# Attention, SoLU mixture and top-1 experts on one core: gate-and-scale factors made with the weight scales, gathers moved behind the second product, two weight buffers kept free

## The chip, the cores and the metric

One core of one Trainium2 chip runs the whole program. The metric is the time of one execution in device microseconds. Three timed runs of the kernel before are at hand, and one profiled execution.

## What is computed

Three layers follow each other. The change touches the third alone.

```python
# 1: attention within chunks of 64 positions, 4 x 8 heads, 576 positions, head size 64
attn = exp(scores - max) / sum;  out = attn @ v
# 2: h = x @ w_in; solu = h * softmax(h); layer norm over 1024 columns, times g_ln; @ w_out
# 3: top-1 mixture of 8 experts over 2304 tokens of 512 columns
logits = x @ w_gate;  expert = argmax(logits);  gate = softmax(logits)[expert]
h = maximum(x_e @ w1[e], 0)        # up to 576 tokens of expert e, 512 -> 1024
y = h @ w2[e]                      # 1024 -> 512
out[token] = gate[token] * y       # tokens over the capacity of 576 stay zero
```

## The kernel before

**Layers 1 and 2** go over 18 tiles of 128 tokens. A planner (class `Plan`) writes out their order from costs and due times. The change leaves this part alone; in the profiled execution it ends at about 376 us. It has put the tokens, already normalized, in a table `xrows` in device memory, and the list of each expert's tokens with their gate values in `idx_sb` (its float view is `gm`).

**Layer 3** goes over 16 weight matrices in the order of `mats`: w1 of experts 0 and 1, w2 of experts 0 and 1, and then w1 and w2 of each expert from 2 to 7. The loop at L1515 takes them one after the other; a turn with w1 is called the *first product* of its expert, and one with w2 its *second product*. The order within a turn is the order in which the code is written, on each engine for itself. An engine goes through its own list in order, and waits on semaphores for the others.

A matrix of 2 MB is handled in four quarters of 512 KB, in buffers that are handed round in a list `free`:

- `load_q` (L1272) takes a free buffer and loads a quarter into it, on SP's queue.
- `norm_q` (L1281) squares and sums a quarter, the even ones on ACT (L1046), the odd ones on DVE (L1044).
- `fin_q` (L1284) adds the four sums up with a small matmul, reduces the result on DVE (`nst`, L136) and makes the scale from it on POOL (`nsb` and `sw`, L141 and L142).
- `split_q` (L1289) splits a quarter into two f16 parts: ACT writes the high part (L1292) into a free buffer, and DVE then writes the low part beside it (L1293), reading the raw quarter and the high part. The raw buffer goes back to `free` after this.

`job` (L1302) says how far ahead each step may run, and that a load is made only where the list holds at least two buffers, so that one is left for the splits. Within a turn, `work(p)` (L1506) asks for the splits of the matrix two turns later, its scale, and the sums of the one three turns later.

**A first product** (L1531 to L1536) runs `emit_span` over the expert's first 256 tokens, in four groups of 24 matmuls with 256 columns (L1398). ACT takes each group's result (`hA`, L1404) and DVE makes its low part (L1405). The second group doesn't start before both have read the first. Further tiles of 128 tokens follow in `emit_b`, under tests of the expert's count of tokens.

**A second product** (L1518 to L1530) has these pieces, in this order:

1. `fetch_all(e + 2)` for experts 2 to 5: for each tile of 128 tokens of the expert after the next a gather on POOL (L1371) from `xrows` into one of four buffers `xga` and `xgb`, and a transposing DMA on SP (L1376) from there. The tiles from the third on stand under tests of the count.
2. `ffac(e)` (L1472), on POOL: gate value times the two matrices' scales for each token of the expert, in `ff`.
3. `emit_d(e, 0)`: 24 matmuls for the first 128 tokens (L324); ACT scales the result by `ff` into `y` (L1460), and POOL scatters its rows to the output (L1461).
4. `work(p)`.
5. `emit_d` for the further tiles, under tests; a last tile of at most 64 rows is scaled on DVE (L1456, L1457).

Then the turn's four weight buffers are released, and up to eight quarters are loaded (L1537, L1538).

Of the kernel before, what the change touches and what calls it, by code (L numbers as in the profile page):

```python
# [23 lines left out]
def attn_solu_top1_moe(  # L24
# [19 lines left out]
    E = w_gate.shape[1]  # L44
# [27 lines left out]
    def small(name, w=1, dtype=F32, bufs=None):  # L72
        return sm.tile([128, w], dtype, tag=name, name=name, **({"bufs": bufs} if bufs else {}))
# [42 lines left out]
    def bank_tile(slot, name):  # L116
        return psp.tile([128, 512], F32, tag=slot, name=name)
# [16 lines left out]
    def tot_reduce(ar):  # L134
        t = small("nst", bufs=8)
        DVE.tensor_reduce(t, ar, AX.X, ALU.add)  # L136
        return t

    def pow_scale(ss, cst, so):
        b = small("nsb", bufs=8)  # L140
        POOL.tensor_scalar(b, ss, 1.0 / cst ** 2, 1e-36, ALU.mult, ALU.add)  # L141
        POOL.tensor_tensor(so, b.to_broadcast([128, 2]), pexp[:, 0:2], ALU.pow)  # L142
# [67 lines left out]
    NORMS = 7  # L210
# [264 lines left out]
    mats = [(0, 0), (0, 1), (1, 0), (1, 1)]  # L475
# [771 lines left out]
    with tc.manual_schedule():  # L1247
# [20 lines left out]
        free = [spare]  # L1268
        raw_q = {(p, qi): raw_m[p][:, qi * WQ:(qi + 1) * WQ] for p in range(3, 7) for qi in range(NQ)}
# [14 lines left out]
        def fin_q(p, qi):  # L1284
            ar = bank_tile("o", "tot")[:, 0:NQ]
            PE.matmul(ar, ones_f, am[:, p, :], start=True, stop=True)
            pow_scale(tot_reduce(ar), CW, sw[:, p, :])

        def split_q(p, qi):  # L1289
            r, s = raw_q.pop((p, qi)), sw[:, p, 0:1]  # L1290
            w = wm_q[p, qi] = free.pop(0).bitcast(F16).rearrange("p (a f) -> p a f", a=2)
            ACT.activation(w[:, 0], r, AF.Copy, scale=s)  # L1292
            DVE.scalar_tensor_tensor(w[:, 1], r, s, w[:, 0], ALU.mult, ALU.subtract)  # L1293
            free.append(r)
# [7 lines left out]
        def job(kind, p, n=1):  # L1302
            for _ in range(n):
                if not todo[kind]:
                    return
                at = todo[kind][0]
                before = todo.get(needs[kind])
                if at[0] >= p + ahead[kind] or (before and before[0][0] <= at[0] and kind != "N"):
                    return
                if kind == "N" and at not in raw_q or kind == "L" and len(free) < 2:  # L1310
                    return
                steps[kind](*todo[kind].pop(0))

        def need(p):
            for kind in "NFS":
                while todo[kind] and todo[kind][0][0] <= p:
                    steps[kind](*todo[kind].pop(0))
# [4 lines left out]
        def release(p):  # L1322
            if p < 3:
                t = wm[p].rearrange("p a f -> p (a f)").bitcast(F32)
                free.extend(t[:, qi * WQ:(qi + 1) * WQ] for qi in range(NQ))
            else:
                free.extend(wm_q.pop((p, qi)).rearrange("p a f -> p (a f)").bitcast(F32) for qi in range(NQ))
# [5 lines left out]
        def fetch_from(e, j, end=NTJ):  # L1333
            if j < end:
                with tc.If(units(e, 2 * j)):
                    fetch(e, j)
                    fetch_from(e, j + 1, end)

        def emit_from(step, e, j, p, end=NTJ):
            if j < end:  # L1340
                with tc.If(units(e, 2 * j)):
                    hT = hT_of(e, j, step)
                    if step is emit_b and e < 2:
                        fetch(e, j)
                    if rows(j) <= 64:
                        step(e, j, p, hT, True)
                    else:
                        with tc.If(units(e, 2 * j + 1)) as full:
                            step(e, j, p, hT, False)
                            emit_from(step, e, j + 1, p, end)  # L1350
                        with full.Else():
                            step(e, j, p, hT, True)
# [6 lines left out]
        def fetch(e, j, again=False):  # L1359
            col, r = e * NTJ + j, rows(j)  # L1360
            xg = xg_n()
            if again:
                xT = bp.tile([128, 2, FF], F16, tag="hc", name="gxTr").rearrange("p a f -> p (a f)")
                xT = xT[:, 0:2 * KD * r].rearrange("p (k c) -> p k c", k=2 * KD)
            elif e < 2:
                xT = gx[e][:, j - 2, 0:2 * KD * r].rearrange("p (k c) -> p k c", k=2 * KD)
            elif j < 2:
                xT = gx[e][:, :, 128 * j:128 * j + 128]
            else:
                xT = bp.tile([128, 2 * KD, r], F16, tag=f"gxT{j}", name=f"gxT{j}")  # L1370
            POOL.indirect_dma_start(  # L1371
                out=xg[0:r, :], out_offset=None, in_=xrows[:, :],
                in_offset=bass.IndirectOffsetOnAxis(ap=idx_sb[0:r, col, 0:1], axis=0),
                bounds_check=NT, oob_is_err=False,
            )
            SP.dma_start_transpose(out=xT, in_=xg[0:r].bitcast(F16))  # L1376
            xT_m[e, j] = xT
# [4 lines left out]
        def fetch_all(e):  # L1382
            gx[e] = bp.tile([128, 2 * KD, 256], F16, tag="gxA", name="gxA")
            fetch(e, 0)
            fetch(e, 1)
            fetch_from(e, 2)
# [54 lines left out]
        def emit_d(e, j, p, hT, half):  # L1441
            col, r = e * NTJ + j, 64 if half else rows(j)
            op = bank_tile(f"tr{tr_n()}", "op2")
            y = bp.tile([128, DM], F32, tag="y", name="y")[0:r]
            s = ff[0:r, col:col + 1]
            if half:
                h = KF // 2
                if j < 2:
                    lhs = lambda a, kk: hT[:, a * KF + kk, 0:64]
                else:  # L1450
                    hT = hT.rearrange("p k c -> p (k c)")[:, 0:KF * 128].rearrange("p (k c) -> p k c", k=KF)
                    lhs = lambda a, kk: hT[:, a * h + kk % h, kk // h * 64:kk // h * 64 + 64]
                mm_half([op[0:64], op[64:128]], lhs, h, weights(p), DM, (0, 0), (range(h), range(h, KF)))
                t = bp.tile([128, 2, FF], F16, tag="hc", name="yt").rearrange("p a f -> p (a f)").bitcast(F32)[0:64, 0:DM]
                ACT.copy(t, op[64:128])
                DVE.tensor_scalar(y, op[0:64], s, None, ALU.mult)  # L1456
                DVE.scalar_tensor_tensor(y, t, s, y, ALU.mult, ALU.add)  # L1457
            else:
                mm3([(op[0:r], 0)], hT, KF, weights(p), DM, DM)
                ACT.activation(y, op[0:r], AF.Copy, scale=s)  # L1460
            POOL.indirect_dma_start(  # L1461
                out=out_v[col], out_offset=bass.IndirectOffsetOnAxis(ap=idx_sb[0:r, col, 0:1], axis=0),
                in_=y, in_offset=None, bounds_check=NT - 1, oob_is_err=False,
            )
# [6 lines left out]
        def ffac(e):  # L1471
            POOL.tensor_scalar(ff[:, e * NTJ:(e + 1) * NTJ], gm[:, e * NTJ:(e + 1) * NTJ, 1],  # L1472
                               sw[:, mats.index((0, e)), 1:2], sw[:, mats.index((1, e)), 1:2], ALU.mult, ALU.mult)

        fetch_all(2)
        ffac(0)
        job("S", 2, 4)
        job("L", 2, 1)
        y = bp.tile([128, DM], F32, tag="y", name="ye")
# [26 lines left out]
        def work(p):  # L1506
            job("S", p, NQ)
            job("F", p)
            job("N", p, NQ)
            job("S", p, NQ)  # L1510
# [4 lines left out]
        for p in range(2, NM):  # L1515
            a, e = mats[p]
            need(p)
            if a == 1:  # L1518
                if 1 < e < E - 2:
                    fetch_all(e + 2)  # L1520
                if p > 2:
                    ffac(e)
                if p > 2:
                    emit_d(e, 0, p, hT_m[e, 0], False)
                work(p)
                emit_from(emit_d, e, 1, p)
                if e == 0:
                    spill(1)
                    emit_from(emit_b, 1, 2, 1)
                    release(1)  # L1530
            else:  # L1531
                hA = bp.tile([128, 2 * KF, 256], F16, tag="hA", name="hA", bufs=1)
                hT_m[e, 0], hT_m[e, 1] = hA[:, :, 0:128], hA[:, :, 128:256]
                emit_span(gx[e], 256, p, hA)
                work(p)
                emit_from(emit_b, e, 2, p)  # L1536
            release(p)  # L1537
            job("L", p, 2 * NQ)  # L1538
# [27 lines left out]
```

## Time and profile before

| | us |
|---|---|
| timed runs | 698.91, 695.51, 696.09 |
| median | 696.09 |
| time of the profiled execution | 694.92 |
| its span, from the first to the last instruction | 693.2 |
| TensorE busy | 525.2 (76% of the span) |
| VectorE, ScalarE, GpSimd busy | 381.1, 308.8, 271.9 |
| layer 3, from the first gather to the end | 377 to 693 |

Times within the trace count from the start of the span. Engines are written PE (matmul), DVE, ACT, POOL and SP; SPq and POOLq are the DMA issues of these two. In a row of the timeline stand start, duration, engine, line and operation, the output and its inputs by the program's names, and how many instructions the row takes together; in brackets, how long the engine had been idle before it, and what ended that. Layer 3's turns can be told by their matmuls: L1398 with `gxA` is a first product, L324 with `hA` the start of a second one. The tokens are spread unevenly: expert 2 has one tile of 128 tokens, expert 4 has five tiles.

### The profile page before, as it was taken

Reading aid. Unit: us, or ns where it says so; the run is one execution under the profiler, and the core shown is the slowest. Engines: PE = TensorE matmul, PEld = TensorE weight load, DVE = VectorE, ACT = ScalarE, POOL = GpSimd, SP = SyncE. Lnnn points to the kernel's source line nnn. Section 1 sums busy time; section 2 is a strip of 40 time slices with the busy share of each in tenths; the row PEclk is TensorE's granted clock in tenths of the full one; section 3 lists DMA queues with packets and bytes.
Section 4 is the critical chain, followed back from the end, with each engine's and each line's share of the span. In section 5 each row is a group of like instructions: output and inputs, shape, how many; then the busy total and the mean of one; then the engine's idle time right before and its main releaser. Section 6 shows DMA issues by size and latency. Waiting matters only on the chain. (4 is left out here: it accounts for less than half of the span.)

```text
span 693.2 us, 12254 instructions
## 1 busy us (share of the span) xinstructions
PE 525.2 (76%) x4428; PEld 313.9 (45%) x4428; DVE 381.1 (55%) x654; ACT 308.8 (45%) x510; POOL 271.9 (39%) x429
## 2 busy tenths in 40 slices
PE   6567897979899898998778575615838787578794
PEld 6444443534454454444577334314424336254541
DVE  4887978857477456848775324522634323636210
ACT  1556866536575555447422332432534332625110
POOL 1465657542568555667552211110504111513001
PEclk9657999999999999999979798867969899889998
DMA  8993699999975755443554495383271750602021
GB/s 187 341 222 61 125 226 225 235 246 249 191 143 112 138 107 112 95 100 78 188 146 136 108 352 184 110 167 122 69 252 62 162 136 18 139 9 40 11 61 39
DMA packets 186395, 98.84 MB, mean 143 GB/s; under 512 B 167519, under 2 KB 167519, under 8 KB 185920
## 3 DMA queue, kind: packets, MB, share of 16 engines
q1 hardware_dynamic: 180624, 87.23, 52.5%
q0 software_dynamic: 3824, 10.38, 4.6%
q8 instruction: 51, 0.84, 0.5%
q10 hardware_dynamic: 1856, 0.06, 0.2%
q14 instruction: 40, 0.33, 0.1%
HBM read 61.80 MB, written 9.63 MB: 103 GB/s over the span
## 5 line engine op out<-in xcount | busy, mean ns | idle before, releaser
L324 PE MATMUL op<-w_out,uT 128*128 128x512 f16 x432 | 100.1, 390 | 11.1 <-DMA uT<-uc 8.1
L324 PE MATMUL hp<-w_in,xT 128*128 128x512 f16 x432 | 98.3, 385 | 4.9 <-DVE eh L738 2.6
L1398 PE MATMUL hp<-gxA,rawm 128*128 128x256 f16 x360 | 54.4, 293 | 52.9 <-DVE hA L1405 49.0
L1461 POOL DMA_INDIRECT out_dram<-y,idx_sb x20 | 22.9, 1144 | 131.0 <-ACT y L1460 83.0
L324 PEld LDWEIGHTS <-uT 128*128 128x128 f16 x432 | 42.5, 100 | 63.0 <-DMA uT<-uc 9.1
L324 PEld LDWEIGHTS <-xT 128*128 128x128 f16 x432 | 42.0, 99 | 53.7 <-issue 5.2
L1398 PEld LDWEIGHTS <-rawm 128*128 128x128 f16 x360 | 37.6, 105 | 62.5 <-issue 51.7
L1405 DVE SCALAR_TENSOR_TENSOR hA<-hp,hA 128x512 f16<-128x512 f32 x24 | 16.6, 691 | 62.9 <-ACT hA L1404 62.7
L1404 ACT ACTIVATE hA<-hp 128x512 f16<-128x512 f32 x24 | 14.3, 597 | 70.6 <-PE hp L1398 70.1
L1293 DVE SCALAR_TENSOR_TENSOR rawm<-rawm,sw 128x1024 f16<-128x1024 f32 x21 | 27.0, 1284 | 33.0 <-ACT rawm L1292 33.0
L141 POOL TENSOR_SCALAR nsb<-nst 128x1 f32<-128x1 f32 x19 | 8.3, 436 | 89.9 <-DVE nst L136 86.1
L324 PEld LDWEIGHTS <-hA 128*128 128x128 f16 x240 | 23.7, 102 | 35.6 <-issue 9.0
L1398 PEld LDWEIGHTS <-wm 128*128 128x128 f16 x264 | 26.2, 115 | 22.5 <-issue 16.8
L1398 PE MATMUL hp<-gxA,wm 128*128 128x256 f16 x168 | 27.7, 294 | 10.6 <-DVE hA L1405 10.6
L1292 ACT ACTIVATE rawm<-rawm,sw 128x1024 f16<-128x1024 f32 x21 | 24.0, 1145 | 23.8 <-DVE rawm L1293 12.3
L324 PE MATMUL op<-wm,hA 128*128 128x512 f16 x126 | 30.3, 392 | 5.0 <-issue 3.8
L765 POOL TENSOR_TENSOR uc<-eh,uc 128x1024 f16<-128x1024 f32 x13 | 28.4, 2186 | 12.6 <-ACT uc L760 12.6
L1460 ACT ACTIVATE y<-op,ff 128x512 f32<-128x512 f32 x15 | 10.1, 680 | 48.4 <-POOL ff L1472 24.8
L1044 DVE SCALAR_TENSOR_TENSOR dumpv<-rawm 128x1024 f16<-128x1024 f32 x22 | 28.7, 1303 | 4.0 <-DMA rawm<-in_moe_w_dram 3.7
L760 ACT CAST uc<-eh 128x1024 f16<-128x1024 f32 x18 | 18.8, 1045 | 24.1 <-POOL eh L756 11.4
L324 PE MATMUL op<-rawm,hA 128*128 128x512 f16 x114 | 28.2, 396 | 0.6 <-ACT hA L1404 0.6
L142 POOL TENSOR_TENSOR sx<-nsb,pexp 128x2 f32<-128x2 f32 x36 | 27.3, 759 | 3.0
(270 smaller groups left out, 1175.5 us busy)
## 6 DMA issues: line engine op xcount, KB each, us to landing
rawm<-in_moe_w_dram SPq DMA_DIRECT2D x46, 512.0 KB, 5.3
wm<-in_moe_w_dram SPq DMA_DIRECT2D x17, 512.0 KB, 5.3
vt<-in_v_dram SPq DMA_DIRECT2D x72, 64.0 KB, 2.8
xrows<-xr SPq DMA_DIRECT2D x18, 256.0 KB, 2.8
qt<-in_q_dram SPq DMA_DIRECT2D x16, 256.0 KB, 3.7
kt<-in_k_dram SPq DMA_DIRECT2D x16, 256.0 KB, 4.6
rawd<-in_moe_w_out_dram SPq DMA_DIRECT2D x8, 512.0 KB, 5.2
rawd<-in_moe_w_in_dram SPq DMA_DIRECT2D x3, 1024.0 KB, 7.4
```

What stands on the lines that cost most here:

```text
L142: POOL.tensor_tensor(so, b.to_broadcast([128, 2]), pexp[:, 0:2], ALU.pow)
L324: PE.matmul(pp, xT[:, a * K + kk, :], wslice(w, b_, kk * N + f0, n0), start=(kk == 0 and a == 0 and b_ == 0), stop=(kk == K - 1 and a == 1),)
L760: ACT.copy(uc[:, 0, :], st["eh", t])
L765: eng.tensor_tensor(uc[:, 1, :], st.pop(("eh", t)), uc[:, 0, :], ALU.subtract)
L1044: DVE.scalar_tensor_tensor(dumpv, r, 1.0, r, ALU.mult, ALU.mult, accum_out=acc)
L1292: ACT.activation(w[:, 0], r, AF.Copy, scale=s)
L1293: DVE.scalar_tensor_tensor(w[:, 1], r, s, w[:, 0], ALU.mult, ALU.subtract)
L1398: PE.matmul(hp[:, m, :], wslice(weights(p), b_, kk * FF + (i * g + m) * 128, 128), xT[:, a * KD + kk, :], start=(kk == 0 and b_ == 0 and a ...
L1404: ACT.activation(hi, hp, AF.Relu)
L1405: DVE.scalar_tensor_tensor(h[:, KF + i * g:KF + (i + 1) * g, :], hp, 0.0, hi, ALU.max, ALU.subtract)
L1460: ACT.activation(y, op[0:r], AF.Copy, scale=s)
L1461: POOL.indirect_dma_start(out=out_v[col], out_offset=bass.IndirectOffsetOnAxis(ap=idx_sb[0:r, col, 0:1], axis=0), in_=y, in_offset=None, b ...
```

## The change

Three edits, all in layer 3.

1. The factors are made as soon as the second matrix's scale is there: `fin_q` calls `ffac` behind `pow_scale`. For the matrices whose scales come from the planner's part (experts 0, 1 and 2) the factors are made together at the start. The call of `ffac` in the second product goes.
2. `fetch_all(e + 2)` is called at the end of the second product, behind the last tile, and no more at its start.
3. A load is made only where three buffers are free, so that two are left.

```diff
@@ fin_q
             pow_scale(tot_reduce(ar), CW, sw[:, p, :])
+            if mats[p][0]:
+                ffac(mats[p][1])
@@ job
-                if kind == "N" and at not in raw_q or kind == "L" and len(free) < 2:
+                if kind == "N" and at not in raw_q or kind == "L" and len(free) < 3:
                     return
@@ before the loop
         fetch_all(2)
-        ffac(0)
+        for p in range(2, NORMS):
+            if mats[p][0]:
+                ffac(mats[p][1])
@@ the loop, second product
             if a == 1:
-                if 1 < e < E - 2:
-                    fetch_all(e + 2)
-                if p > 2:
-                    ffac(e)
                 if p > 2:
                     emit_d(e, 0, p, hT_m[e, 0], False)
                 work(p)
                 emit_from(emit_d, e, 1, p)
                 if e == 0:
                     spill(1)
                     emit_from(emit_b, 1, 2, 1)
                     release(1)
+                if 1 < e < E - 2:
+                    fetch_all(e + 2)
```

On POOL, at the start of expert 2's second product, this stood before: the gathers for expert 4, the factors of expert 2, the first scatter (`out_dram`), and the scale of the next matrix.

```order
L1371 DMA xgb<-xrows,idx_sb 128x512 x2
...
L1371 DMA xga<-xrows,idx_sb 128x512
...
L1371 DMA xgb<-xrows,idx_sb 64x512
...
L1472 TENSOR_SCALAR ff<-idx_sb,sw 128x5
L1461 DMA out_dram<-y,idx_sb 2304x512
L141 TENSOR_SCALAR nsb<-nst 128x1
L142 TENSOR_TENSOR sw<-nsb,pexp 128x2
```

And this stands there now (lines are two further down in the changed file):

```order
L1463 DMA out_dram<-y,idx_sb 2304x512
L141 TENSOR_SCALAR nsb<-nst 128x1
L142 TENSOR_TENSOR sw<-nsb,pexp 128x2
L1474 TENSOR_SCALAR ff<-idx_sb,sw 128x5
...
L1373 DMA xgb<-xrows,idx_sb 128x512 x2
...
L1373 DMA xga<-xrows,idx_sb 128x512
...
L1373 DMA xgb<-xrows,idx_sb 64x512
```

The scatter, the scale and the factors (now those of expert 3) come first, the other tiles' scatters follow where rows are left out, and the gathers come last, ahead of the scale that the next first product asks for.

On SP's queue, over the end of expert 2's first product and its second product, this stood before: loads, the transposes for expert 4, loads.

```order
L1276 DMA rawm<-in_moe_w_dram 128x2x512
L1276 DMA wm<-in_moe_w_dram 128x2x512
L1276 DMA rawm<-in_moe_w_dram 128x2x512 x2
L1376 DMA_TRANSPOSE gxA<-xgb 128x8x128 x2
...
L1376 DMA_TRANSPOSE gxT_6527<-xgb 128x8x64
...
L1276 DMA wm<-in_moe_w_dram 128x1024 x2
L1276 DMA rawm<-in_moe_w_dram 128x1024 x2
```

And this stands there now:

```order
L1276 DMA rawm<-in_moe_w_dram 128x1024
L1276 DMA rawm<-in_moe_w_dram 128x2x512
L1276 DMA wm<-in_moe_w_dram 128x2x512 x2
...
L1378 DMA_TRANSPOSE gxA<-xgb 128x8x128 x2
...
L1378 DMA_TRANSPOSE gxT_6876<-xgb 128x8x64
...
L1276 DMA wm<-in_moe_w_dram 128x2x512
L1276 DMA rawm<-in_moe_w_dram 128x1024
L1276 DMA wm<-in_moe_w_dram 128x1024 x2
```

SP's own order stays loads, transposes, loads; what has moved is when the transposes' gathers are issued, and each group of four loads begins with the last quarter of the matrix before.

## Rows read from the trace of the kernel before

**Rows 1.** Stretches: core, us, busy PE, PEld, DVE, ACT, POOL, PE clock, DMA share, GB/s

```profile
415.60:440.00 24.40, 12.86 (x99) 10.20 (x98) 9.21 (x10) 7.74 (x10) 4.98 (x5) 0.84 0.52 180
440.00:450.20 10.20, 8.49 (x26) 3.28 (x27) 6.42 (x9) 4.96 (x7) 0.00 (x0) 0.72 0.18 66
450.20:485.30 35.10, 12.51 (x99) 10.33 (x100) 9.73 (x12) 10.01 (x14) 3.31 (x5) 0.71 0.58 147
571.60:586.80 15.20, 11.14 (x101) 9.62 (x99) 4.27 (x8) 3.71 (x6) 0.93 (x1) 1.00 0.09 27
```

**Rows 2.** Waits from 400 to 693 us: who waited for whom, us, times, longest

```profile
PE hp L1398 <- DVE hA L1405: 59.6, 12, 20.5
```

**Rows 3.** Timeline from 440 to 475 us, all engines: expert 2's second product, expert 3's first

```profile
446.82 0.38 SPq L1276 DMA_DIRECT2D rawm<-in_moe_w_dram  x1
...
448.84 7.21 SPq L1376 DMA_TRANSPOSE gxA<-xgb  x2
...
450.01 0.16 DVE L136 TENSOR_REDUCE nst<-tot 128x1 f32<-128x4 f32 x1 [0.81 <-PEq L1341]
...
458.08 0.96 POOL L1371 DMA_INDIRECT xgb<-xrows,idx_sb  x1 [21.30 <-DMA gxA<-xgb]
...
459.46 0.69 ACT L1460 ACTIVATE y<-op,ff 128x512 f32<-128x512 f32 x1 [11.77 <-POOL ff L1472]
...
461.62 0.18 POOL L141 TENSOR_SCALAR nsb<-nst 128x1 f32<-128x1 f32 x1
...
462.65 1.15 ACT L1292 ACTIVATE rawm<-rawm,sw 128x1024 f16<-128x1024 f32 x1 [0.28 <-POOL sw L142]
...
471.33 1.28 DVE L1293 SCALAR_TENSOR_TENSOR wm<-wm,sw 128x1024 f16<-128x1024 f32 x1 [1.22 <-ACTq L1341]
...
473.52 1.87 PE L1398 MATMUL hp<-gxA,rawm 128*128 128x256 f16 x8 [20.54 <-DVE hA L1405]
```

**Rows 4.** Timeline from 586 to 610 us: expert 5's second product, expert 6's first

```profile
589.86 2.19 ACT L1292 ACTIVATE rawm<-wm,sw 128x1024 f16<-128x1024 f32 x2 [1.58 <-POOL sw L142]
...
593.45 2.48 DVE L1293 SCALAR_TENSOR_TENSOR wm<-rawm,sw,wm 128x1024 f16<-128x1024 f32 x2
...
598.42 0.69 ACT L1460 ACTIVATE y<-op,ff 128x512 f32<-128x512 f32 x1 [4.29 <-POOL ff L1472]
...
609.70 1.44 PE L1398 MATMUL hp<-gxA,rawm 128*128 128x256 f16 x6 [10.73 <-DVE hA L1405]
```

**Rows 5.** Timeline from 400 to 425 us: expert 1's second product, expert 2's first

```profile
404.32 2.36 PE L324 MATMUL op<-spare,hT 128*128 128x512 f16 x6 [2.49 <-DVEq L1341]
...
406.48 4.87 PE L324 MATMUL op<-rawm,hT 128*128 128x512 f16 x18
...
412.14 0.69 ACT L1460 ACTIVATE y<-op,ff 128x512 f32<-128x512 f32 x1 [8.77 <-POOL ff L1472]
...
424.77 0.80 PE L1398 MATMUL hp<-gxA,wm 128*128 128x256 f16 x3 [6.37 <-DVE hA L1405]
```

**Rows 6.** Timeline from 499 to 541 us: expert 3's second product, expert 4's first

```profile
500.19 0.78 POOL L141 TENSOR_SCALAR nsb<-nst 128x1 f32<-128x1 f32 x1
...
502.80 1.15 ACT L1292 ACTIVATE rawm<-wm,sw 128x1024 f16<-128x1024 f32 x1 [1.82 <-POOL sw L142]
...
513.85 1.44 PE L1398 MATMUL hp<-gxA,rawm 128*128 128x256 f16 x6 [10.67 <-DVE hA L1405]
...
540.83 2.77 PE L1412 MATMUL hp<-rawm,gxT 128*64 128x512 f16 x12 [5.19 <-DVE hc L1438]
```

**Rows 7.** Timeline from 550 to 575 us: expert 4's second product

```profile
563.65 1.46 PE L324 MATMUL op<-rawm,hT 128*128 128x512 f16 x6 [2.38 <-ACT y L1460]
```

**Rows 8.** Timeline from 620 to 694 us: half tile of expert 6's first product

```profile
620.90 1.49 PE L1412 MATMUL hp<-rawm,gxT 128*64 128x512 f16 x12
```

**Rows 9.** The tile xga in layer 3: DMAs that write or read it

```profile
DMA to landing us min/median/max: 3.1/4.0/5.0
```

**Rows 10.** DMA issues: KB each, median us from issue to landing

```profile
wm<-in_moe_w_dram SPq DMA_DIRECT2D x17, 512.0 KB, 5.3
```

## The prediction

> **What bounds the kernel now.** I read the stretches of layer 3 first, then its waits, then the timeline around each long wait of PE. The stretches show what an undisturbed first product takes: 15.20 us for expert 5, PE at its full clock (1.00, which is 2.4 GHz) and busy for 11.14 us of them. The same work takes 24.40 us for expert 2 and 35.10 us for expert 3, at mean clocks of 0.84 and 0.71 [rows 1]. So PE is not the limit here; it stands still. The waits name the place: the second group of a first product waited 59.6 us for DVE's low part of the first group, 20.5 us of it at once [rows 2]. A wait of 1.4 us belongs there each time, as the undisturbed product has it too.
>
> The timeline of expert 3 shows what makes DVE late [rows 3]. Read it backwards. PE goes on at 473.52, after the last low part of a split (471.33 + 1.28). Those four splits began at 462.65, right behind their scale; its first step on POOL was at 461.62, though the sums had been there at 450.01. POOL had been in the gathers of the expert after next: the fifth waited 21.30 us, until 458.08, for a transpose to empty its buffer. The transposes were late because SP issues in order, and the load ahead of them, at 446.82, waited for a buffer that the previous splits gave back. Behind the gather stood the factors, and ACT waited 11.77 us for them with its output `y`. Two things lie on this path: POOL's order and the pace of the splits.
>
> **The pace of the splits (two buffers free).** With one buffer free each split writes where the one before has just been read, so ACT and DVE take turns: from 462.65 to 472.61, 9.96 us for four [rows 3]. Late in the layer, when all loads are done and five buffers are free, ACT runs ahead and DVE never waits: from 589.86 to 595.93, 6.07 us [rows 4]. With two, the third split on ACT waits for the first on DVE, and the fourth for the second. DVE's part is the longer one (1.28 against 1.15 us), so after its first it still has no gap: 1.15 + 4 x 1.28 is 6.3 us with the row's first durations, 6.2 with the 1.24 that it has when running on (2.48 for two). I take 6.2, so 3.75 us less for each set; the bounds are the two measured paces. Two buffers are nearer to five than to one, since what makes the turns is that there is no second buffer.
>
> **What each place is worth,** on the clock of the kernel before.
>
> 1. *Expert 1's second product to expert 2's first* [rows 5]. PE began at 404.32, freed by DVE's passing a branch behind the splits of the turn before; these end 3.75 us sooner, of which at most the 2.49 us of idleness can be won, and at least nothing. Half, 1.2 us. Its 24 matmuls end at 406.48 + 4.87 = 411.35, and `y` came at 412.14, behind the factors: 0.8 us. The splits behind it: 3.75 us. The wait of 6.37 us then shrinks to 2.4 or less, and after a wait of that length PE went on at its full clock (6 matmuls in 1.46 us [rows 7]). So expert 2's first product needs 11.14 us of PE where it needed 12.86 [rows 1]: 1.7 us. Together 7.4 us.
> 2. *Expert 2's second product to expert 3's first* [rows 3]. `y` no longer waits for the factors: 11.77 us, less 0.4 that I take for PE's own last result. The scale then falls beside DVE's two sums of squares. Beside idle DVE the step from `nsb` to the splits took 1.03 us (461.62 to 462.65), beside such sums 2.61 us (500.19 to 502.80 [rows 6]). I take the dearer: 11.3 - 1.6 = 9.7 us. It can't start before the sums at 450.01, and 461.62 - 11.3 is just behind that. With the splits' 3.75 us, 13.4 us.
> 3. *Expert 3's second product to expert 4's first* [rows 6]. No gather is in the way here. The splits ahead of `y` and of the sums end 3.75 us sooner, and the next set, from 502.80, takes 3.75 us less: 7.5 us of the 10.67 that PE waited (and of 3.11 at the start of the turn).
> 4. *Expert 4's half tile*. PE waited 5.19 us for a low part behind a set of splits: 3.75 us. The wait left is below 2 us, so the clock stays up: its first 12 matmuls took 2.77 us [rows 6] where expert 6's took 1.49 [rows 8], 1.3 us. Together 5.0 us.
> 5. *Expert 4's second product*. The 2.38 us for a `y` behind four splits go [rows 7]: 2.4 us.
> 6. *Expert 5's second product to expert 6's first* [rows 4]. The splits have their pace already. `y` waited 4.29 us for the factors, and the scale becomes dearer by 1.6 us beside the sums: 2.7 us.
>
> The sum is 7.4 + 13.4 + 7.5 + 5.0 + 2.4 + 2.7 = 38.4 us. The profiled execution took 694.92 us, 1.2 us below the median of 696.09; I take the sum from the median: 657.7 us, and write 657.5.
>
> **What the moved and added pieces cost.** The factors of experts 3 to 7 stand behind a scale, in time in which POOL waits for the next `y`; three at the start, each 0.35 us, lie ahead of a scatter that waits anyway. I cost them at nothing; without that cover they are 0.35 us each. The gathers come behind the last scatter. Their landing takes 4.0 us [rows 9], and two transposes took 7.2 us beside loads [rows 3]. They are read two turns later, more than 25 us away. On POOL they stand ahead of the next scale, which is asked for at the end of the next first product, 15 us on. The fifth gather for expert 4 waits until the first transpose is done, 4.0 + 3.6 us after the first gather: that hides too, since SP's loads ahead are done by then. SP's loads of the turn come behind the transposes and up to 12 us later; their quarters are squared three turns on (the last quarter of each matrix, loaded a turn later now, two). What is late next is still the low part of the first group, by some 6 us, for experts 3, 4 and 6.
>
> The trace shows the scale at 1.03 us beside idle DVE and at 2.61 us beside sums that read two tensors. The Trainium skill, page "SBUF — State Buffer", section "Who interferes with whom", says that a DVE instruction with two SBUF inputs contends with a GpSimd instruction that reads SBUF, and that the loser blocks until the other ends; the two rows agree. It speaks against this change, which packs DVE's splits and sums tighter around POOL's scale. Taken in full, an estimate from that page, each of POOL's two instructions could lose one DVE instruction, 2.5 us at places 2 and 6 in place of my 1.6: 659.5 us; without the rule it would be 654.3.
>
> **The rivals.**
> - *The splits keep their turns.* If the third split must wait as the second does now, places 3 to 5 give nothing, and what is left is 0.8 + 9.7 + 2.7 = 13.2 us: 682.9 us. For it: no set in the trace runs on two buffers. Against it: on five, ACT runs two ahead and no more. Chance 0.10.
> - *POOL is held at its new place.* Should the fifth gather wait 21.3 us again, it begins 5 us behind the scale (four gathers of 1.3 us) and ends 26 us behind, and the next scale, due after a first product of 15.2 us, is 11 us late: 668.5 us. For it: SP is in order. Against it: the load that held SP waited for splits which now end before the gathers. Chance 0.07.
> - *Slower: the read-ahead of the weights breaks.* Loads now stand behind transposes of gathers that wait for the last `y`. If the squares had to wait for them, each of the four second products with gathers would cost 4.0 + 7.2 + 5.3 = 16.5 us (the load's own landing [rows 10]), 66 us in all against 38.4: 724 us. It decides once a quarter is asked for within that time of its issue; now two turns, over 30 us, lie between, and no sum of squares in layer 3 stands in the list of waits with a DMA. Chance 0.03.
> - *Nothing is won.* `y` and the splits could turn out to be held by something that the profile puts down to the factors, such as POOL's passing of the branches: 696 us. Against it: the splits' turns are plain in the rows. Chance 0.02.
>
> **How the numbers follow.** The forecast has the rest, 0.78. Its own lower end: PE's start at place 1 in full (1.3 us more), the scale at its cheap price twice (3.2), expert 2's second product at full clock (8.49 us of PE at 0.72 [rows 1], of which nearly 3 go), and the restarts behind the three waits left at full clock (12.51 against 11.14 us, 1.4 each): 657.5 - 11.6 is about 646 us. The upper end takes in the first two rivals: 683 us. A measurement of this kernel tells about 0.5% from no change, 3.5 us, as its runs lie that far apart. All cases but two are faster by more than this: faster 0.95, the same 0.02, slower 0.03.
>
> **What would show it.** In the changed profile a set of four splits takes 6 to 6.5 us from experts 2 on, and no `y` waits for the factors. PE's wait for the first group's low part falls from 20.5 to 6 or 7 us at expert 3, from 10.7 to 6 or 7 at expert 4, and from 59.6 to some 30 us in all. A gather waits at most 5 us for a transpose. The forecast is wrong if the sets still take 10 us, if POOL's `nsb` waits behind a gather, or if sums of squares wait for weights.

## The result, and the profile after

The changed kernel took 656.92 us (median of four runs, 652.29 to 666.63), the kernel before beside it 696.3 us. The ratio is 0.9406, with a 95% interval from 0.9330 to 0.9482; it leaves out disturbed, slower executions (those that were profiled of e1 and e11 below are two of them), so the medians named here, which hold all executions, can stand up to one per cent beside it. 657.5 us was forecast. The profiled execution took 654.07 us. From here on lines of the changed file are two further down (L1400 for L1398, L1407 for L1405, and so on).

The page, its first line and PE's:

```profile
span 652.4 us, 12259 instructions
...
PE 520.7 (80%) x4428; PEld 313.7 (48%) x4428; DVE 379.7 (58%) x654; ACT 308.2 (47%) x510; POOL 272.0 (42%) x429
```

The engines do the same work. Of the 40.8 us of span that are gone, 36.3 are time in which PE stood, and 4.5 are PE's own (525.2 us busy before, 520.7 now). Stretches of the first products of experts 2, 3 and 6 (columns as in [rows 1]):

```profile
413.12:430.68 17.56, 12.64 (x98) 10.19 (x97) 6.79 (x9) 5.19 (x8) 0.93 (x1) 0.90 0.73 275
...
440.37:461.24 20.87, 15.13 (x98) 11.58 (x99) 8.16 (x9) 6.51 (x8) 8.39 (x7) 0.78 0.74 187
...
557.16:585.24 28.08, 17.16 (x122) 12.57 (x123) 13.16 (x19) 10.52 (x15) 9.76 (x11) 0.76 0.43 90
```

Expert 2's took 24.40 us before and expert 3's 35.10 [rows 1]. Expert 6's took 27.4 us before (from 596.18 to PE's next turn at 623.61) and has gained nothing; both stretches hold the half tile as well. The waits from 380 us on:

```profile
PE hp L1400 <- DVE hA L1407: 33.5, 12, 8.8
...
POOL xgb L1373 <- DMA gxA<-xgb: 3.1, 1, 3.1
```

59.6 us have become 33.5 and the longest is 8.8 in place of 20.5 [rows 2]; `y` behind the factors no longer stands in the list. The waits at experts 3, 4 and 6 are 4.18, 6.53 and 8.80 us, where 6 or 7 at experts 3 and 4 were forecast. The timeline from expert 2's second product to expert 3's first shows how the wait there fell:

```profile
437.14 0.69 ACT L1462 ACTIVATE y<-op,ff 128x512 f32<-128x512 f32 x1 [0.27 <-ACTq L1343]
...
439.32 0.95 POOL L141 TENSOR_SCALAR nsb<-nst 128x1 f32<-128x1 f32 x1
440.36 1.72 POOL L142 TENSOR_TENSOR sw<-nsb,pexp 128x2 f32<-128x2 f32 x1
...
442.11 1.15 ACT L1294 ACTIVATE rawm<-rawm,sw 128x1024 f16<-128x1024 f32 x1 [2.06 <-POOL sw L142]
...
446.99 1.28 DVE L1295 SCALAR_TENSOR_TENSOR wm<-rawm,sw,wm 128x1024 f16<-128x1024 f32 x1
...
449.82 3.47 PE L1400 MATMUL hp<-gxA,rawm 128*128 128x256 f16 x16 [4.18 <-DVE hA L1407]
...
453.66 0.96 POOL L1373 DMA_INDIRECT xgb<-xrows,idx_sb  x1 [3.10 <-DMA gxA<-xgb]
```

The scale begins 1.5 us behind the end of `y`, ahead of all gathers, and the four splits take 442.11 to 448.27, 6.16 us in place of 9.96 [rows 3]. The fifth gather waits 3.10 us, behind everything that matters. All eight sets that took 9.96 to 10.04 us from 394 us on now take 6.15 to 6.24.

### The profile page after: what moved, and what is told of

Same layout as the page of the kernel before. It is cut to its first block, busy times and chain, and to the rows that moved or that the text cites. A ratio compares the mean times of both kernels' runs of the same rounds, so it can differ in the third digit from the quotient of the medians.

```text
span 652.4 us, 12259 instructions
## 1 busy us (share of the span) xinstructions
PE 520.7 (80%) x4428; PEld 313.7 (48%) x4428; DVE 379.7 (58%) x654; ACT 308.2 (47%) x510; POOL 272.0 (42%) x429
## 5 line engine op out<-in xcount | busy, mean ns | idle before, releaser
L324 PE MATMUL op<-w_out,uT 128*128 128x512 f16 x432 | 100.5, 391 | 10.3 <-DMA uT<-uc 6.6
L1400 PE MATMUL hp<-gxA,rawm 128*128 128x256 f16 x360 | 57.6, 305 | 19.1 <-DVE hA L1407 16.3
L324 PEld LDWEIGHTS <-uT 128*128 128x128 f16 x432 | 42.7, 100 | 62.6 <-issue 10.3
L1407 DVE SCALAR_TENSOR_TENSOR hA<-hp,hA 128x512 f16<-128x512 f32 x24 | 16.6, 691 | 66.9 <-ACT hA L1406 60.8
L1400 PEld LDWEIGHTS <-rawm 128*128 128x128 f16 x360 | 39.1, 109 | 29.1 <-issue 17.9
L1400 PE MATMUL hp<-gxA,wm 128*128 128x256 f16 x192 | 32.3, 293 | 17.6 <-DVE hA L1407 17.2
L1400 PEld LDWEIGHTS <-wm 128*128 128x128 f16 x288 | 27.7, 110 | 31.7 <-issue 25.8
L324 PEld LDWEIGHTS <-hA 128*128 128x128 f16 x240 | 23.1, 99 | 29.6 <-ACT hA L1406 1.7
L1295 DVE SCALAR_TENSOR_TENSOR rawm<-rawm,sw 128x1024 f16<-128x1024 f32 x20 | 25.4, 1288 | 11.6 <-ACT rawm L1294 11.5
L744 ACT ACTIVATE dump<-eh,nmu 128x1024 f16<-128x1024 f32 x18 | 20.6, 1147 | 18.0 <-POOL nmu L741 18.0
L142 POOL TENSOR_TENSOR sx<-nsb,pexp 128x2 f32<-128x2 f32 x36 | 27.4, 760 | 3.0
L696 DVE SCALAR_TENSOR_TENSOR xc<-x,sx,xc 128x512 f16<-128x512 f32 x18 | 17.9, 996 | 17.8 <-ACT xc L691 14.6
```

The lines of the kernel that those rows point to most:

```text
L324: PE.matmul(pp, xT[:, a * K + kk, :], wslice(w, b_, kk * N + f0, n0), start=(kk == 0 and a == 0 and b_ == 0), stop=(kk == K - 1 and a == 1),)
L696: DVE.scalar_tensor_tensor(xc[:, 1, :], st.pop(("x", t)), sx[:, 0:1], xc[:, 0, :], ALU.mult, ALU.subtract)
L744: ACT.activation(dump, st["eh", t], AF.Square, bias=nmu, accum_out=ss)
L1400: PE.matmul(hp[:, m, :], wslice(weights(p), b_, kk * FF + (i * g + m) * 128, 128), xT[:, a * KD + kk, :], start=(kk == 0 and b_ == 0 and a ...
L1407: DVE.scalar_tensor_tensor(h[:, KF + i * g:KF + (i + 1) * g, :], hp, 0.0, hi, ALU.max, ALU.subtract)
```

## The experiments

Each run has its own runs of the kernel before on the same chip; a time "by the ratio" is the ratio times their median.

**1. The edits one by one.** Run e1 is the third edit alone (`len(free) < 3`), e2 the first alone, e3 the second alone, e4 the first and second:

```diff
# e1, against the kernel before
-... kind == "L" and len(free) < 2:
+... kind == "L" and len(free) < 3:
# e2: the hunks of fin_q and of the start; ffac(e) taken out of the second product
# e3: fetch_all(e + 2) from the start to the end of the second product; ffac(e) stays at its start
# e4: both of these, with len(free) < 2
```

> Only the third edit: two buffers left free, factors and gathers where they stood. My theory (two separate mechanisms, the pace of the splits and POOL's order): each set of four splits from expert 2 on takes 6.2 us instead of 9.96, worth about 5 to 7 us at the first place, 3.75 to 7.5 at the second, 7.5 at the third, 5.0 and 2.4 at the fourth and fifth and nothing at the sixth, 25 to 29 us in all: 667 to 671 us. The fifth gather for expert 4 still stands ahead of the factors, and PE's wait at expert 3's first product stays above 12 us. Rival (the gathers held POOL only because the splits were late, so that the pace alone frees both): the time comes down to that of all three edits, 657 us or less.

> Only the first edit: the factors behind the scale of the second matrix. My theory (what holds y at experts 2 and 5 is the gathers in POOL's queue, and the next scale stands behind them too): y no longer waits for the factors, but the scale behind the gathers begins at most 1 to 2 us earlier at places 2 and 6; with 0.8 us at place 1 the whole is 2 to 4 us: 692 to 694 us. Rival (the factors themselves hold the path, as the waits of y name them, 24.8 us in all): 10 to 13 us of these are won, 683 to 686 us.

> Only the second edit: the gathers at the end of the second product; the factors, at its start as before, are then the first on POOL there. My theory: 9.7 us at place 2 and 2.7 at place 6, and nothing at place 1: 684 us, with sets of splits at 9.96 us. Rival (the factors hold the path wherever the gathers are): 693 us or more. Rival (POOL is held at the new place, since the loads ahead of the transposes still wait for buffers that the slow splits give back): a gather waits over 10 us for a transpose there, and the time is 690 us or more.

> The first and second edit without the third (one buffer left free). My theory: 0.8 + 9.7 + 2.7 = 13.2 us, 683 us, with sets of splits at 9.96 us; the third edit on top of it is then worth some 26 us, as by itself. Rival (the edits only work together): less than 5 us, 691 us or more. Rival (the pace of the splits does not matter, the order is all): 657 to 662 us.

Measured: e1 0.9614 (0.9535 to 0.9694), 669.5 us by the ratio; e2 0.9974 (0.9932 to 1.0015), no difference that can be told; e3 0.9860 (0.9784 to 0.9936), 686.7 us; e4 0.9822 (0.9766 to 0.9878), 684.0 us. All four lie within 3 us of the theory's numbers, and none at a rival's. The interval of e3 alone reaches up to a rival's time (692 us); its trace speaks against both rivals, as no gather waits over 3.3 us for a transpose there, and `y` waits for the factors once only, at expert 1. The pace of the splits carries two thirds of the gain and POOL's order one third. In e2 the queue shows why moving the factors out alone does nothing: the gather that held them holds the scatter and the scale instead.

```profile
461.29 0.96 POOL L1373 DMA_INDIRECT xgb<-xrows,idx_sb  x1 [22.51 <-DMA gxA<-xgb]
462.56 1.05 POOL L1463 DMA_INDIRECT out_dram<-y,idx_sb  x1 [0.31 <-issue]
463.69 0.18 POOL L141 TENSOR_SCALAR nsb<-nst 128x1 f32<-128x1 f32 x1
```

In e1, with fast splits, the same gather still waits, and PE with it (POOL, then PE at expert 3's first product):

```profile
460.34 0.96 POOL L1371 DMA_INDIRECT xgb<-xrows,idx_sb  x1 [20.65 <-DMA gxA<-xgb]
...
471.98 3.29 PE L1398 MATMUL hp<-gxA,rawm 128*128 128x256 f16 x15 [17.60 <-DVE hA L1405]
```

**2. All three again, and all but the first.** e5 is the changed kernel on the chip of the next three runs. e12 leaves the factors in the second product:

```diff
# e12, against the changed kernel
@@ fin_q
-            if mats[p][0]:
-                ffac(mats[p][1])
@@ the loop, second product
+                if p > 2:
+                    ffac(e)
                 if p > 2:
                     emit_d(e, 0, p, hT_m[e, 0], False)
```

> The kernel with all three edits once more, to stand beside the next three on one chip. 652 to 660 us. If the edits add up from their own parts (the buffers alone, and factors with gathers), the ratio to the kernel before is 0.9614 + 0.9822 - 1 = 0.944; if they depend on each other it is well below that.

> The second and third edit without the first (factors at the start of the second product, as before). My theory (with the gathers gone from there, the factors are the first thing on POOL in their turn; only expert 1's y waits for them, and of that wait no more than about 1 us is beyond PE's own last result): 1 to 2 us more than all three edits, 657 to 662 us, ratio 0.941 to 0.948. Rival (the waits of y that name the factors are paid in full, 7.7 us at expert 1): 664 us or more, ratio 0.95 or more.

e5: 658.4 us, ratio 0.9427 (0.9363 to 0.9490), what the parts add up to (0.944). e12: 665.81 us, 0.9518 (0.9444 to 0.9592). That is the rival's number, 6 us above all three edits by the ratios, though the two intervals overlap and e12's reaches into the theory's range as well; the trace has to decide. It shows at expert 1's second product:

```profile
410.49 1.04 POOL L1461 DMA_INDIRECT out_dram<-y,idx_sb  x1 [10.62 <-ACTq L1341]
...
411.98 4.05 PE L324 MATMUL op<-rawm,hT 128*128 128x512 f16 x18
...
419.88 0.35 POOL L1472 TENSOR_SCALAR ff<-idx_sb,sw 128x5 f32<-128x5 f32 x1 [8.36 <-DMA xga<-xrows,idx_sb]
420.27 0.69 ACT L1460 ACTIVATE y<-op,ff 128x512 f32<-128x512 f32 x1 [10.06 <-POOL ff L1472]
...
429.09 1.23 PE L1398 MATMUL hp<-gxA,wm 128*128 128x256 f16 x5 [4.88 <-DVE hA L1405]
```

PE's result was there at 416.03, and `y` came 4.2 us later, not 0.8 as the theory had it, nor the 7.7 of the rival; the splits stand behind `y` on ACT. In e5 `y` starts with PE's end (412.13), and PE's wait is 1.41 us. From the first matmul of expert 1's second product to PE's restart are 18.4 us in e12 and 14.8 in e5.

Where each edit pays, by place: the time from PE's first matmul of the place to that of the next, in the profile of the kernel before less that of the run (us). Place 3 ends, and place 4 begins, with the first 512-column matmul of expert 4's first product. "Other" is all outside the six places.

| place | forecast | the change | e5 | e12 | e1 buffers | e4 order | e3 gathers |
|---|---|---|---|---|---|---|---|
| 1 | 7.4 | 8.6 | 9.5 | 4.3 | 1.9 | 3.6 | 3.2 |
| 2 | 13.4 | 14.7 | 13.7 | 14.4 | 5.7 | 6.0 | 6.5 |
| 3 | 7.5 | 6.8 | 6.2 | 6.9 | 7.1 | -1.0 | -0.8 |
| 4 | 5.0 | 5.7 | 5.7 | 5.7 | 5.7 | -0.4 | -0.3 |
| 5 | 2.4 | 3.6 | 3.6 | 3.6 | 2.5 | 1.1 | 1.1 |
| 6 | 2.7 | -1.8 | 0.3 | -1.9 | -0.9 | -0.3 | -0.3 |
| other | 0 | 3.1 | -2.9 | -4.3 | -3.7 | -2.0 | -4.9 |

The last row is the spread of the program itself: expert 1's second product began between 403.6 and 413.9 us in the fourteen profiles, behind code that hardly differs, and the stretch behind place 6 took 66.8 to 70.2 us in the runs of this table and the kernel before. So small differences between single profiles are read by place, not by span. Place 1 of the kernel before is itself such a case: e3 changes nothing there and has 3.2 us less, so it is the better measure. Against e3, the buffers without the factors are worth -1.3 (e1) and 1.1 us (e12) there, the factors without the buffers 0.4 (e4), and both together 5.4 and 6.3. Each of these is a difference of single profiles.

**3. Are two buffers enough?** e6 keeps three (`len(free) < 4`).

> All three edits, with three buffers left free in place of two. My theory (two are enough: a set is bound by DVE's four parts as soon as ACT is not held by the first of them): sets of 6.06 in place of 6.16 us, less than 1 us in all, and no wait for weights, since a quarter is squared more than 20 us after its load: 653 to 660 us, the same as with two. Rival (every buffer kept free costs read-ahead): a wait of sums of squares for a load, or a longer wait of PE, and over 662 us.

0.9423 (0.9347 to 0.9498), the same as e5; the sets take 6.05 us. A third buffer has nothing left to win that the time would show, as DVE's low parts run on almost without a gap with two.

**4. What makes the scale dear?** In e7 `work` asks for the splits ahead of the sums:

```diff
-            job("N", p, NQ)
             job("S", p, NQ)
+            job("N", p, NQ)
```

> All three edits, and within a turn the sums of squares stand behind the splits in place of between scale and splits. My theory (POOL's scale is slowed by DVE's sums with two inputs beside it): the two POOL steps take about 1.0 us in place of the 2.2 to 2.8 that they have beside the sums, and the splits begin 1.2 to 1.8 us earlier behind their sum; but DVE's two sums (2.4 us) now stand ahead of the low part for which PE waits, so that the time is the same or up to 6 us slower: 654 to 663 us. Rival (the scale is slow for another reason): it stays at 2.2 to 2.8 us, and each of places 1, 2, 3 and 6 loses the whole 2.4 us, 665 us.

0.9525 (0.9458 to 0.9592), 667.2 us: 7 us more than e5 by the ratios, 9 by the medians, and beyond what the theory allowed; the intervals overlap a little, but the slowest run of e5 (661.3 us) lies below the fastest of e7 (662.1). The groups of lines show the scale's two steps and DVE's sums, first the changed kernel from 400 us on, then e7 from 430 us on (columns: count, busy, mean ns, idle before and what ended it):

```profile
L142 POOL TENSOR_TENSOR sw<-nsb,pexp 128x2 f32<-128x2 f32 x9 | 13.4, 1492 | 0.8
...
L1044 DVE SCALAR_TENSOR_TENSOR dumpv<-wm 128x1024 f16<-128x1024 f32 x10 | 12.2, 1221 | 0.2
...
L141 POOL TENSOR_SCALAR nsb<-nst 128x1 f32<-128x1 f32 x9 | 6.7, 743 | 32.8 <-DVE nst L136 32.4
```

```profile
L1044 DVE SCALAR_TENSOR_TENSOR dumpv<-wm 128x1024 f16<-128x1024 f32 x10 | 12.2, 1222 | 0.2
...
L142 POOL TENSOR_TENSOR sw<-nsb,pexp 128x2 f32<-128x2 f32 x9 | 6.5, 717 | 0.8
...
L1286 PE MATMUL tot<-am,ones_f 128*128 128x4 f32 x18 | 3.3, 251 | 16.2 <-DVEq L1343 13.2 <-DVE dumpv L1044 3.0
...
L141 POOL TENSOR_SCALAR nsb<-nst 128x1 f32<-128x1 f32 x9 | 1.7, 186 | 32.7 <-DVE nst L136 32.4
```

The mechanism is as the theory had it: without sums beside it the scale takes 0.90 us (0.186 + 0.717) in place of 2.24. The price was looked for in the wrong place. PE waits less for low parts (23.1 us in all, where e5 has 32.5), but the sums now come so late that PE stands 16.2 us ahead of the small matmul `tot` that adds them up; in the changed kernel that idle time is 2.5 us. Neither theory had this wait.

**5. What is left, and a faster version.** In e8 the splits of a second product are spread over the next first product:

```diff
@@ emit_span, behind the low part of each group
+                if between:
+                    between()
@@ work
-            job("S", p, NQ)
+            if not mats[p][0]:
+                job("S", p, NQ)
@@ the loop, first product
-                emit_span(gx[e], 256, p, hA)
+                emit_span(gx[e], 256, p, hA, lambda: job("S", p - 1))
```

> All three edits, and the four splits that stood in the second product, behind y, are spread over the next first product, one behind each group's low part. My theory (what PE still waits for at the first group of experts 3, 4 and 6 are the splits that stand ahead of it on ACT and DVE): these waits, 4.2, 6.5 and 8.8 us in the changed kernel, shrink to the 1.4 us that each first product has anyway, and the restarts at half clock behind them go: 15 to 20 us less, 637 to 642 us. Rival (DVE is full there: the splits only hold the groups behind them in place of the first): the later groups wait instead, and the time stays within 3 us of the changed kernel, 653 to 660 us.

0.9247 (0.9188 to 0.9305), 647.02 us: some 12 us less than e5, where 15 to 20 were expected. PE's wait for low parts from 400 us on:

```profile
PE hp L1400 <- DVE hA L1407: 17.1, 12, 1.6
```

Two rows of PE's timeline:

```profile
480.60 0.49 PE L1400 MATMUL hp<-gxA,wm 128*128 128x256 f16 x3 [3.17 <-ACTq L1343]
...
582.92 5.28 PE L324 MATMUL op<-rawm,hA 128*128 128x512 f16 x12 [4.61 <-ACT wm L1294]
```

Twelve waits of 1.4 us are left, so the mechanism holds: the splits ahead of the low part were the whole of what PE waited for beyond that. The rest of the expected gain went into new waits, two of them shown. Three further orders tried to remove these. e9 puts `work(p)` behind the further tiles in the second products of experts 2 to 7, e11 does so in the first products, e10 in both:

```diff
# e9, second product
-                work(p)
+                if e < 2:
+                    work(p)
                 emit_from(emit_d, e, 1, p)
+                if e > 1:
+                    work(p)
# e11, first product
-                work(p)
                 emit_from(emit_b, e, 2, p)
+                work(p)
```

> The version with spread splits, and in the second products of experts 2 to 7 the scale and the sums of squares stand behind the last tile in place of behind the first. My theory (after the spread, what PE still waits for at the end of expert 3's second product, 3.2 us, is the second tile's y, which stands behind ACT's sums): this wait goes, and the sums (2.5 us of DVE) fall into the 2.6 us of the next first group: 2 to 4 us less than with spread splits alone, 643 to 645 us, ratio 0.919 to 0.922. Rival (the scale, now later, holds the spread splits and with them the later groups of the first product): waits of PE for the second or third group above 1.4 us, and 647 us or more.

> As the run before it, and in the first products, too, scale, sums and splits stand behind the further tiles in place of ahead of them. My theory (the half tile of expert 4 waits 3.0 us and that of expert 6 several us for an activation behind four splits on ACT and DVE): these waits go, but the splits then run beside the next second product, whose y and op banks wait for them instead; 640 to 645 us. Rival (the splits come too late for the second product that needs its own y): 650 us or more.

> The version with spread splits, and only the first products' scale, sums and splits behind the further tiles. By the same theory 2 to 4 us less than spread splits alone, 643 to 645 us; by the rival (y of the next second product behind the splits holds the scatter, the sums and the end of the turn) 647 us or more.

e9: 0.9309 (0.9255 to 0.9364), no gain over e8, a miss. The wait at 480.6 is gone, but others stand at expert 6's first product, for the first and the second group:

```profile
556.08 0.49 PE L1400 MATMUL hp<-gxA,wm 128*128 128x256 f16 x3 [3.21 <-ACT y L1464]
561.88 0.80 PE L1400 MATMUL hp<-gxA,wm 128*128 128x256 f16 x3 [3.02 <-DVE hA L1407]
```

e10: 0.9187 (0.9138 to 0.9236), 639.85 us; e11: 0.9143 (0.9097 to 0.9189), 642.87 us. Their intervals overlap, so which is better stays open; both beat the changed kernel, by 2.4 and 2.8 points against e5. In both, the half tile of expert 4 no longer waits for its activation behind four splits: that stretch (place 4) takes 13.4 us, 16.3 in e8.

## Why the prediction was right, step by step

- **The pace of the splits.** 6.2 us were forecast, 6.16 measured (1.15 + 4 x 1.24, from which the forecast took its 6.2, is 6.1), and e6 shows that a third buffer takes 0.1 us more off a set. Right. The rival that splits keep their turns falls.
- **Place 2**, 13.4 us: 14.7 and 13.7. Right. The scale did become dearer, 2.76 us from the start of `nsb` to the end of `sw`, 1.8 more than in e7, where 1.6 were forecast. e1 and e4 give 5.7 and 6.0 alone, and both together somewhat more than their sum.
- **Places 3, 4 and 5**, 7.5, 5.0 and 2.4: about 6.5, 5.7 and 3.6. Right. e1 has the first two in full, so they are the buffers' alone. Place 5 was 1.2 us short: the wait of PE at the head of expert 5's second product, 1.24 us in the kernel before, went too, and by e3 and e4 (1.1 us each) that belongs to POOL's order.
- **Place 1**, 7.4: 8.6 and 9.5, some 6 us of it by the better measure. The sum held, its parts did not. The factors were put at 0.8 us, read from the kernel before, where PE's own result was late: its clock was 0.50 until 408.10, and its 24 matmuls took 7.03 us, 5.34 in e12. There `y` waits 4.2 us for the factors, and e5 is 5.2 us shorter. The 6.6 us that the forecast gave to the buffers come only with the factors out of the way. The row names a gather as what the factors wait for, but no gather was under way. By the semaphore events in the traces it was the scatter of expert 0's second tile: POOL's step at the branch behind it starts when the scatter has landed. In e12 it was begun at 410.49, had landed at 419.00, and the factors came at 419.88; in the kernel before these are 403.65, 410.88 and 411.76. There most of this wait was hidden behind PE's slow start.
- **Place 6**, 2.7: -1.8 in one profile and 0.3 in the other. Wrong. The rows of the changed kernel:

```profile
555.36 0.69 ACT L1462 ACTIVATE y<-op,ff 128x512 f32<-128x512 f32 x1 [0.25 <-ACTq L1343]
...
557.94 0.50 POOL L141 TENSOR_SCALAR nsb<-nst 128x1 f32<-128x1 f32 x1
558.53 1.70 POOL L142 TENSOR_TENSOR sw<-nsb,pexp 128x2 f32<-128x2 f32 x1
560.26 1.15 ACT L1294 ACTIVATE wm<-wm,sw 128x1024 f16<-128x1024 f32 x1 [2.00 <-POOL sw L142]
...
568.74 0.80 PE L1400 MATMUL hp<-gxA,wm 128*128 128x256 f16 x3 [8.80 <-DVE hA L1407]
...
578.08 0.49 PE L1400 MATMUL hp<-gxA,wm 128*128 128x256 f16 x3 [2.12 <-DVE hA L1407]
```

  `y` did stop waiting, and the step from its end to the splits rose from 2.4 us (599.11 to 601.55, where the splits began in the kernel before) to 4.2, about as forecast. PE's wait fell from 10.73 [rows 4] to 8.80 us. But the clock behind it was 0.50 again, to 572.40, and its mean over this product is 0.76. In the first profile it fell a second time, to 0.50 from 579.40 to 582.70, behind the 2.12 us, and PE needed 16.5 us from its restart to the next turn where the kernel before had 13.9; e5, where it fell once, needed 14.5. The forecast had no term for that. Besides, some 1.1 us of what is won here is counted at place 5, since PE's turn itself begins that much sooner.
- **POOL held at its new place** falls: the gather waits 3.1 us. **The read-ahead breaks** falls: no sum of squares waits for a load, and even with three buffers (e6) none costs anything that the time shows.
- **The clock at place 1.** Full speed behind the restart was forecast. In e5 it held (wait 1.41 us); in the first profile, behind a wait of 2.03 us, it did not (0.50 from 418.95 to 422.30, 0.90 over the product). So the one row from which the forecast took this, a wait of 2.38 us, does not settle it.
- **The sum.** That 657.5 stands so close to 656.92 is luck in part. Against the forecast the first profile has 0.7 to 1.3 us more at each of places 1, 2, 4 and 5, 0.7 less at place 3, 4.5 less at place 6, and 3.1 more outside the six places, where the profile of e5 has 2.9 less. By the ratio the time is 654.9 us.

## What to carry to other kernels

Where two engines work a ring of buffers, look at how many are free when a batch begins: with one, the second engine's read holds the first engine's write, and the pair runs at the sum of both times (9.96 us for four here) instead of the longer one (6.16); here one more buffer was enough. An in-order queue is read by what stands behind a waiting instruction, not by the name in the wait: here the row said "factors", and moving the factors alone gave nothing; where the factors were the ones to wait (e12), the row said "gather" for a scatter. A wait that seems covered by 1 us should be priced again on the timeline that the other edits make, since its cover may be what they remove.

## What had not been expected

- Beside DVE's sums POOL alone paid: the sums take 1.22 us each with the scale beside them and without, the scale 2.24 and 0.90 in all. The timeline of the changed kernel shows POOL held to the end of each sum or longer:

```profile
547.74 1.22 DVE L1044 SCALAR_TENSOR_TENSOR dumpv<-rawm 128x1024 f16<-128x1024 f32 x1
...
547.91 1.09 POOL L141 TENSOR_SCALAR nsb<-nst 128x1 f32<-128x1 f32 x1 [7.89 <-DVE nst L136]
...
549.00 1.23 DVE L1044 SCALAR_TENSOR_TENSOR dumpv<-wm 128x1024 f16<-128x1024 f32 x1
...
549.09 1.72 POOL L142 TENSOR_TENSOR sw<-nsb,pexp 128x2 f32<-128x2 f32 x1
```

  `nsb` ends at 549.00, the first sum at 548.96; `sw` ends 0.58 us behind the second. The Trainium skill, page "SBUF — State Buffer", section "Who interferes with whom", says that the order of issue decides who blocks; the trace agrees, as DVE's sum started first both times. The forecast's estimate from that page, a whole sum for each of POOL's two steps, 2.5 us, is more than was lost: 1.3 us on average, and 1.9 here (2.8 against 0.9).
- The sums of squares slow the scale by 1.3 us, and still cost less there than behind the splits (e7).
- The start of expert 1's second product differs by up to 10.3 us between executions whose code up to there is nearly the same, more than most terms of the sum.
